# Grouped-query attention and a residual MLP on one core: where the next batch's attention is threaded into the MLP, and in what portions

## The chip, the core and the metric

The kernel runs on one core of a Trainium2 chip. Its engines run side by side, each through its own list of instructions: TensorE (PE; its weight loads are shown as PEld), VectorE (DVE), ScalarE (ACT), GpSimd (POOL) and SyncE (SP). POOL and SP issue nearly all the transfers. The metric is the device time of one launch in microseconds, as the median of several runs.

## The reference

Eight batches are independent of one another. Each is an attention with 16 query heads and 4 key/value heads (384 positions, head width 64), followed by a mixing block over positions and an MLP over 1024 channels with 4096 hidden ones.

```
attention:  scores = q @ k.T / 8 ;  attn = softmax(scores) ;  x = attn @ v      # 16 heads, 4 share one k, v
a1 = alpha1 * x + beta1
u  = x + lam * (w_tok @ a1)            # mixes the 384 positions
a2 = alpha2 * u + beta2
out = u + lam * (relu(a2 @ w_ch1) @ w_ch2)     # 1024 -> 4096 -> 1024
```

Inputs and outputs are float32; the matmul operands are bfloat16 on the chip.

## The kernel before

**The main work of a pass.** A pass b is the MLP of batch b. `main(b)` issues it as two halves. The first half is the hidden layer: 32 tiles `nt` of 128 hidden channels, each 8 matmuls of 384 columns over the input tiles `dt` (line 413), with ReLU by ACT for even tiles and by DVE for odd ones into `hT` (lines 421 and 423). Its weights come in 16 chunks of two tiles through a ring of five buffers; the load of chunk c+5 is issued by POOL when chunk c is done (line 128). The second half is the output layer: six tiles (`dw`, `ms`), each 32 matmuls of 512 columns (line 448), then two DVE operations `o` (lines 453 and 454) and a store issued by SP (line 455). Both halves use two PSUM banks with the tag "mm" in turn.

**The side work.** The attention and the mixing of batch b+1, `side(b+1)`, are cut into pieces and issued between the main matmuls of pass b. `main` is a generator: it yields after every four matmuls, and at a yield the caller may issue one piece. The pieces are, for a pair p of heads (8 pairs):

- `scores(i)`: one group of four 128x128 score tiles for both heads of a pair (line 202). 18 groups hold the batch's 72 tile pairs. The contraction is 64 wide, so the two heads use the upper and the lower 64 rows of the array. ACT takes the exponential of a whole group, 128x1024 (line 211), into one of four buffers `es`. `scores2(j)` issues two groups in one piece; the exponential of the second is put on the list `late`, which is emptied a little later.
- `av_piece(p, hh)`: the product with v for one head, nine matmuls of 65 columns (line 237). After the second head DVE takes the reciprocal of the sums and scales (lines 242 and 243), then computes a1 (lines 250 and 252).
- `tok(p)`: the mixing over positions, nine matmuls of 128 columns (line 259), and on DVE the sum u and a2 (lines 266 and 270).
- `a2_transpose(p)`: a transposing transfer, issued by SP, writes a2 into `a2T` for the next pass (line 282). For batch 1 the last two pairs go over TensorE. `tok_flip` is `tok` and this.

In the passes from the second on the pieces are spread over the whole pass: nine slots of `scores2`, 16 of `av_piece`, 8 of `tok_flip`. The rule is one line, with `span` 0.95 and `lead` 0 there: a piece is issued when its share of the list is due by the time worked off.

```
if done < len(us) and done * t_all * span < len(us) * (t - t_all * lead):
```

The PSUM for scores is a tag "sc" with two buffers of two banks each; "av" and "tp" have one bank each.

**Inputs of batch b+2.** During pass b, SP loads k at the start (`load_k`). At 55% of the pass POOL copies k into its place (line 101) and issues the loads of q and v (`load_next`, lines 110 and 105). At 85% SP issues two transposing transfers, `flip_k` into `kT` (line 113) and `flip_q` into `qT` (line 117). In the first pass the order is different: the loads for batch 2 are issued at the end of the first half, and the flips at 75%. `kT`, `qT`, the staged q and the placed k have one buffer each.

The order on every engine is the order in which the program issues; no scheduler moves anything (`manual_schedule`).

Of the kernel before, what the change touches and what calls it, by code (L numbers as in the profile page):

```python
# [12 lines left out]
def kernel(  # L13
# [21 lines left out]
    nc = tc.nc  # L35
# [12 lines left out]
    P = 128  # L48
# [14 lines left out]
    sb = ST(tc.tile_pool(name="sb", bufs=2))  # L63
    psum = ST(tc.psum_pool(name="psum", bufs=2))

# [49 lines left out]

    def flip_q(b):
        nc.sync.dma_start_transpose(out=qT.rearrange("p a j s -> p (a j) s"),
                                    in_=qrs[b].rearrange("p h st d -> p (h st d)"))

# [11 lines left out]
    def load_w2(dw, i, n):  # L131
        r, cs = slice(i * NNT // n, (i + 1) * NNT // n), slice(dw * 512, (dw + 1) * 512)
        nc.gpsimd.dma_start(out=w2[:, r, cs], in_=w2src[:, r, cs])  # L133

    def tp_ps(shape, tag="tp"):
        return psum.tile(shape, bf, tag=tag, name="tp", bufs=2 if tag == "mm" else 1)

# [8 lines left out]
    def h_part(nts, dts):  # L146
        for nt in nts:
            if nt % 2 == 0 and nt not in early:
                t = psum.tile([P, 2, 512], f32, tag="sc", name="h", bufs=2)
                early[nt], early[nt + 1] = t[:, 0], t[:, 1]  # L150
            for dt in dts:
                nc.tensor.matmul(out=early[nt][:, :S + 1], lhsT=w1_tiles[nt // CW][:, dt, nt % CW * P:(nt % CW + 1) * P],  # L152
                                 rhs=a2Ts[0][:, dt, :S + 1], start=(dt == 0), stop=(dt == NDT - 1))
# [4 lines left out]
    def side(b):  # L158
# [6 lines left out]
        first = b == 0  # L165
        pe_flip = b < 2

# [14 lines left out]
        def q_transpose(p, n=2, tag="tp", eng="DVE"):  # L182
            src = qrs[1][:, 2 * p:2 * (p + n)] if b else qgs[2 * p // G][:, 2 * p % G:2 * p % G + 2 * n]
            src = src.rearrange("p h st d -> p (h st d)")
            f = src.dtype == f32
            ps = psum.tile([P, n * NST, P], src.dtype, tag=tag, name="tp", bufs=2 if tag == "mm" else 1)
            for i in range(n * NST):
                nc.tensor.matmul(out=ps[:, i, :], lhsT=src[:, i * P:(i + 1) * P], rhs=ident_f if f else ident,
                                 is_transpose=True, start=(i == 0), stop=(i == n * NST - 1), skip_group_check=True)
            evac(eng)(out=qT[:, p:p + n].rearrange("p a j s -> p (a j) s"), in_=ps)  # L190
# [3 lines left out]
        def scores(i, later=False):  # L194
            sc = psum.tile([P, 2, 4, P], f32, tag="sc", name="sc", bufs=2)
            k = 4 * i
            while k < 4 * i + 4:
                n = min(4 * i + 4, k - k % NST + NST) - k
                p, sk, st = k // (NST * NST), k // NST % NST, k % NST
                for hh in range(2):  # L200
                    r = slice(hh * D, (hh + 1) * D)
                    nc.tensor.matmul(out=sc[:, hh, k % 4:k % 4 + n], lhsT=kT[r, sk, 2 * p // G, :],  # L202
                                     rhs=qT[r, p, st:st + n, :], start=True, stop=True)
                k += n

            def exp():
                if first:
                    e = hTf[:, i % 6 * 1024:(i % 6 + 1) * 1024].rearrange("p (h k s) -> p h k s", h=2, k=4)
                else:
                    e = sb.tile([P, 2, 4, P], bf, tag="es", name="es", bufs=EB)  # L210
                nc.scalar.activation(out=e, in_=sc, func=EXP, scale=scale_qk)  # L211
                ess[i] = e

            if later:
                late.append(exp)
            else:
                exp()

        def scores2(j):
# [3 lines left out]
            scores(2 * j + 1, True)  # L223

        def av_piece(p, hh):
            while late:
                late.pop(0)()
            if hh == 0:
                avs[p] = psum.tile([P, 2, NST, D1], f32, tag="mm" if first else "av", name="av",
                                   bufs=2 if first else 1)  # L230
            av = avs[p]
# [22 lines left out]
        def tok(p):  # L254
            tag, n = ("mm", 2) if first else ("av", 1) if pe_flip else ("tp", 1)
            ps = psum.tile([P, NST, P], f32, tag=tag, name="tok", bufs=n)
            for tt in range(NST):
# [14 lines left out]
        def a2_transpose(p):  # L272
            if first:
                ps = psum.tile([P, NST, P], f32, tag="tp" if p % 2 else "av", name="ut", bufs=1)
                for tt in range(NST):
                    nc.tensor.matmul(out=ps[:, tt, :], lhsT=x[:, tt, cols(p)], rhs=ident_f, is_transpose=True,
                                     start=(tt == 0), stop=(tt == NST - 1), skip_group_check=True)
                nc.scalar.activation(out=a2T[:, p, :S], in_=ps.rearrange("p a b -> p (a b)"),
                                     func=mybir.ActivationFunctionType.Copy, scale=al2T[:, p:p + 1])
                return  # L280
            if not pe_flip or p < 6:
                nc.sync.dma_start_transpose(
# [21 lines left out]
        def rows_r(tag):  # L304
            ps = psum.tile([P, 512], f32, tag=tag, name="r", bufs=1)
            for st in range(NST):
# [13 lines left out]
        def spread(ps_, vs, tag, eng="DVE"):  # L320
            n = len(ps_)
            ps = psum.tile([P, 4, P], f32, tag=tag, name="vec", bufs=1)
            w = vs[1] - vs[0]
# [8 lines left out]
        def add(f, *a):  # L332
            us.append(lambda: f(*a))

        def tok_flip(p):
            tok(p)
            a2_transpose(p)

        if not first:
            if pe_flip:  # L340
                add(split, 2, 4)
                add(k_transpose, 0)
                add(q_transpose, 0, 2, "av")
                add(k_transpose, 2)
                add(q_transpose, 2, 2, "av")
            for j in range(NP + 4):
# [3 lines left out]
                if j <= NP:  # L350
                    add(scores2, j)
                    if pe_flip and j in (1, 3):
                        add(q_transpose, 4 + 2 * (j // 2))
                if 2 < j < NP + 3:
                    add(tok if pe_flip else tok_flip, j - 3)
                if pe_flip and j > 3:
                    add(a2_transpose, j - 4)
                if pe_flip and j < 2:
# [3 lines left out]
                elif j < 2:  # L362
                    us.extend([lambda: None] * 2)
            return us
# [4 lines left out]
        lower, upper = range(NP // 2), range(NP // 2, NP)  # L369
        def av(p):  # L370
            av_piece(p, 0)
            av_piece(p, 1)

        ut = a2_transpose
# [27 lines left out]
    def main(b):  # L402
# [3 lines left out]
        for c in range(NCH):  # L406
            w1 = w1_tiles.pop(b * NCH + c)
            for j in range(CW):
                nt = c * CW + j
                begun = b == 0 and nt in early  # L410
                ps = early[nt] if begun else psum.tile([P, 512], f32, tag="mm", name="h", bufs=2)
                for dt in range(0 if begun else NDT):
# [27 lines left out]
        for dw in range(NDW):  # L440
            cs = slice(dw * 512, (dw + 1) * 512)
            for ms in range(NST):
                ps = psum.tile([P, 512], f32, tag="mm", name="ch", bufs=2)
                o = sb.tile([P, 512], f32, tag="tmp", name="o", bufs=4)
# [16 lines left out]
    with tc.manual_schedule(engines=order):  # L461

        def warmup(n):
            warm = psum.tile([P, 512], f32, tag="mm", name="warm", bufs=2)
            for _ in range(n):
# [97 lines left out]
        for b in range(B):  # L563
            us = side(b + 1) if b + 1 < B else []
            half = False
            done, t, loaded, flipped = 0, 0, b == 0 or b + 2 >= B, b + 2 >= B
            lead, span = (0.04, 0.82) if b == 0 else (0, 0.95)
            if b + 2 < B:
                load_k(b + 2)
            for dt in main(b):  # L570
                t += dt
                half = not half
                if late and half:
                    late.pop(0)()
                if done < len(us) and done * t_all * span < len(us) * (t - t_all * lead):
                    us[done]()
                    done += 1
                if not loaded and t > t_all * 0.55:
                    loaded = True
                    load_next(b + 2)  # L580
                if not flipped and t > t_all * (0.85 if b else 0.75):
                    flipped = True
                    flip_k(b + 2)
                    flip_q(b + 2)
            while done < len(us):
                us[done]()
                done += 1


# [28 lines left out]
```

The softmax here doesn't subtract the row's maximum and nothing guards it: scores larger than these inputs give would overflow.

## Time and profile before

| | us |
|---|---|
| median of 7 runs | 811.53 (810.67 to 813.43) |
| the profiled execution: device time | 814.55 |
| its span, first to last instruction | 812.4 |
| PE busy | 797.9 (98% of the span) |
| DVE, ACT, POOL busy | 343.6, 226.1, 178.0 |
| DMA engines, mean busy share by 40ths of the span | mostly 90% or more, less in the second half of each pass |

The profiled execution took 2.15 us more than its span, and 3.02 us more than the median of the runs. A pass from the third to the sixth takes 97.4 us in the trace; the last one, which has no side work, 84.5 us from its first matmul to the end of the table's window. The granted TensorE clock has a mean of 0.998.

### The profile page before, as it was taken

Reading aid. Unit: us, or ns where it says so; the run is one execution under the profiler, and the core shown is the slowest. Engines: PE = TensorE matmul, PEld = TensorE weight load, DVE = VectorE, ACT = ScalarE, POOL = GpSimd, SP = SyncE. Lnnn points to the kernel's source line nnn. Section 1 sums busy time; section 2 is a strip of 40 time slices with the busy share of each in tenths; the row PEclk is TensorE's granted clock in tenths of the full one; section 3 lists DMA queues with packets and bytes.
Section 4 is the critical chain, followed back from the end, with each engine's and each line's share of the span. In section 5 each row is a group of like instructions: output and inputs, shape, how many; then the busy total and the mean of one; then the engine's idle time right before and its main releaser. Section 6 shows DMA issues by size and latency. Waiting matters only on the chain.

```text
span 812.4 us, 14107 instructions
## 1 busy us (share of the span) xinstructions
PE 797.9 (98%) x6076; PEld 450.6 (55%) x6129; DVE 343.6 (42%) x669; ACT 226.1 (28%) x311; POOL 178.0 (22%) x232
## 2 busy tenths in 40 slices
PE   8999999999999999999999999999999999999997
PEld 4766554565456654566455655556545565456545
DVE  7645552344433444344452444424444244432122
ACT  6654211332113321233103331034211432102100
POOL 6234320324002330123201340022500321003000
PEclk9999999999999999999999999999999999999999
DMA  9999999999169992799947997499935999129611
GB/s 186 197 207 200 205 200 185 155 170 167 36 137 182 178 134 69 137 171 170 127 96 129 173 180 87 113 141 163 188 69 103 154 173 127 37 66 184 88 40 40
DMA packets 233550, 112.96 MB, mean 139 GB/s; under 512 B 82952, under 2 KB 227344, under 8 KB 233488
## 3 DMA queue, kind: packets, MB, share of 16 engines
q0 software_dynamic: 170736, 83.47, 82.8%
q1 hardware_dynamic: 62208, 28.20, 15.4%
q8 instruction: 48, 0.79, 0.4%
q10 hardware_dynamic: 544, 0.39, 0.1%
q14 instruction: 14, 0.11, 0.1%
HBM read 170.53 MB, written 12.58 MB: 225 GB/s over the span
## 4 chain that ended last, share of the span: by engine, by line
PE 85%; DMA 9%; DVE 4%; issue 1%; POOL 1%; ACT 0%; SPq 0%; POOLq 0%; DVEq 0%
PE h L413 36%; PE ch L448 36%; DMA w<-in_moe_w_ch_dram 6%; PE av L237 4%; PE sc L202 4%; PE tok L259 4%; DMA q_raw<-in_q_dram 2%; DVE x L243 1%; DVE hT L423 1%; PE h L152 1%; DMA a2T<-a 1%; DVE a1f L250 0%; DVE a L252 0%; PE warm L466 0%; POOL w L133 0%
## 5 line engine op out<-in xcount | busy, mean ns | idle before, releaser
L413 PE MATMUL h<-a2T,w 128*128 128x384 bf16 (+1 forms) x2016 | 351.4, 327 | 1.0 <-DVE hT L423 0.3
L448 PE MATMUL ch<-w,hT 128*128 128x512 bf16 (+2 forms) x1547 | 345.3, 370 | 4.3 <-issue 1.0
L413 PEld LDWEIGHTS <-w 128*128 128x128 bf16 x2016 | 190.0, 98 | 126.9 <-issue 10.7
L448 PEld LDWEIGHTS <-hT 128*128 128x128 bf16 x1600 | 146.3, 98 | 154.1 <-issue 5.8
L128 POOL DMA_DIRECT2D w<-in_moe_w_ch_dram x128 | 112.3, 879 | 542.2 <-PE h L413 504.7
L211 ACT ACTIVATE es<-sc 128x1024 bf16<-128x1024 f32 x126 | 123.4, 1021 | 290.9 <-PE sc L202 290.9
L423 DVE TENSOR_SCALAR hT<-h,bias 128x384 bf16<-128x384 f32 x128 | 79.0, 617 | 190.7 <-PE h L413 190.1
L421 ACT ACTIVATE hT<-h,bias 128x384 bf16<-128x384 f32 x128 | 74.3, 581 | 204.8 <-PE h L413 204.3
L453 DVE TENSOR_TENSOR o<-ch,vecs 128x512 f32<-128x512 f32 (+2 forms) x50 | 33.3, 666 | 91.1 <-PE ch L448 91.1
L266 DVE TENSOR_TENSOR x<-tok,x 128x384 f32<-128x384 f32 x64 | 35.5, 555 | 80.2 <-PE tok L259 77.9
L237 PEld LDWEIGHTS <-es 128*128 128x128 bf16 x1008 | 45.8, 97 | 20.5
L237 PE MATMUL av<-v,es 128*128 128x65 bf16 x1008 | 49.0, 193 | 0.0
L202 PE MATMUL sc<-qT,kT 64*128 64x384 bf16 (+2 forms) x576 | 45.7, 273 | 1.7 <-DMA qT<-q_raw 1.6
L259 PEld LDWEIGHTS <-wtokT 128*128 128x128 bf16 x576 | 37.8, 98 | 13.8 <-DVE x L243 1.6
L242 DVE RECIPROCAL rinv<-av 128x6 f32<-128x6 f32 x64 | 12.3, 192 | 71.1 <-PE av L237 70.9
L259 PE MATMUL tok<-a,wtokT 128*128 128x128 bf16 x504 | 37.3, 219 | 0.0
L243 DVE TENSOR_TENSOR x<-av,rinv 128x384 f32<-128x384 f32 x64 | 35.7, 557 | 2.2
L202 PEld LDWEIGHTS <-kT 64*128 64x128 bf16 x576 | 19.9, 94 | 29.6 <-issue 25.1
L454 DVE TENSOR_TENSOR o<-o,x 128x512 f32<-128x512 f32 (+2 forms) x50 | 33.5, 670 | 1.7
L270 DVE TENSOR_TENSOR a<-x,vecs 128x384 bf16<-128x384 f32 x56 | 31.6, 565 | 1.9
L252 DVE TENSOR_TENSOR a<-a1f,vecs 128x384 bf16<-128x384 f32 x56 | 31.4, 561 | 2.2
L250 DVE TENSOR_TENSOR a1f<-x,vecs 128x384 f32<-128x384 f32 x56 | 31.4, 561 | 1.9
(75 smaller groups left out, 195.6 us busy)
## 6 DMA issues: line engine op xcount, KB each, us to landing
w<-in_moe_w_ch_dram POOLq DMA_DIRECT2D x138, 512.0 KB, 8.0
out_dram<-o SPq DMA_DIRECT2D x47, 256.0 KB, 2.4
q_raw<-in_q_dram POOLq DMA_DIRECT2D x28, 192.0 KB, 7.1
kst<-in_k_dram SPq DMA_DIRECT2D x16, 192.0 KB, 3.4
w<-in_moe_w_ch_dram POOLq DMA_DIRECT2D x1, 2048.0 KB, 16.8
v<-in_v_dram POOLq DMA_DIRECT2D x24, 64.0 KB, 6.8
w<-in_moe_w_ch_dram POOLq DMA_DIRECT2D x4, 256.0 KB, 10.4
a2T<-a SPq DMA_TRANSPOSE x54, 2.3
```

The source lines that it names most:

```text
L128: nc.gpsimd.dma_start(out=t, in_=w1src[:, :, c * CW * P:(c + 1) * CW * P])
L202: nc.tensor.matmul(out=sc[:, hh, k % 4:k % 4 + n], lhsT=kT[r, sk, 2 * p // G, :], rhs=qT[r, p, st:st + n, :], start=True, stop=True)
L211: nc.scalar.activation(out=e, in_=sc, func=EXP, scale=scale_qk)
L237: nc.tensor.matmul(out=av[:, hh, sq, :], lhsT=ess[k // 4][:, m % 2, k % 4, :], rhs=vb[:, sk, hk, :], start=(sk == 0), stop=(sk == NST - 1))
L243: nc.vector.tensor_tensor(out=x[:, :, cols(p)].rearrange("p st (h d) -> p h st d", h=2), in0=av[:, :, :, :D], in1=rinv.to_broadcast([P, 2, ...
L259: nc.tensor.matmul(out=ps[:, tt, :], lhsT=wtokT[:, st, tt * P:(tt + 1) * P], rhs=a1s[p][:, st, :], start=(st == 0), stop=(st == NST - 1 an ...
L266: nc.vector.tensor_tensor(out=u, in0=ps, in1=u, op=ADD)
L413: nc.tensor.matmul(out=ps[:, :n], lhsT=w1[:, dt, j * P:(j + 1) * P], rhs=a2T[:, dt, :n], start=(dt == 0), stop=(dt == NDT - 1))
L421: nc.scalar.activation(out=hT[:, nt, :], in_=ps[:, :S], func=RELU, bias=c1)
L423: nc.vector.tensor_scalar(out=hT[:, nt, :], in0=ps[:, :S], scalar1=c1, scalar2=0.0, op0=ADD, op1=mybir.AluOpType.max)
L448: nc.tensor.matmul(out=ps[:, lo:hi], lhsT=hT[:, nt, ms * P:(ms + 1) * P], rhs=w2[:, nt, dw * 512 + lo:dw * 512 + hi], start=(nt == 0), sto ...
L454: nc.vector.tensor_tensor(out=o[:, lo:hi], in0=o[:, lo:hi], in1=x[:, ms, c], op=ADD)
```

## The change

For the side work issued in the second and the later passes (the batches from 2 on):

- Nothing is issued in the first half of the pass. From the end of the first half on, the yields are numbered by u (48 more in the six output tiles), and a table tells which pieces stand at which u.
- `scores3` issues three groups in one piece, so there are six slots of scores. In two of the six, the third group's exponential is held back until after the following `av`.
- `av` issues both heads of a pair in one piece, so there are eight slots. `tok_flip` keeps its eight; one of them stands directly behind an `av`.
- The PSUM banks "sc", "av" and "tp" are given back after the first pass and become one ring "threes" of three buffers of two banks. Scores, `av` and `tok` take its buffers in turn.
- `load_k` stands at u=1, `load_next` at u=2, `flip_k` at u=34, and `flip_q` is four transfers of two pairs each at u=36, 37, 42 and 43.

The first pass is as before. The core of the diff:

```diff
-    psum = ST(tc.psum_pool(name="psum", bufs=2))
+    mms = ST(tc.psum_pool(name="mms", bufs=2))
+    lead_banks = ExitStack()
+    psum = lead_banks.enter_context(tc.psum_pool(name="psum", bufs=2))
+    threes = []
...
-    def flip_q(b):
-        nc.sync.dma_start_transpose(out=qT.rearrange("p a j s -> p (a j) s"),
-                                    in_=qrs[b].rearrange("p h st d -> p (h st d)"))
+    def flip_q(b, i=0, n=NP):
+        nc.sync.dma_start_transpose(out=qT[:, i:i + n].rearrange("p a j s -> p (a j) s"),
+                                    in_=qrs[b][:, 2 * i:2 * (i + n)].rearrange("p h st d -> p (h st d)"))
...
+    def three():
+        return threes[0].tile([P, 2, 4, P], f32, tag="sc", name="sc", bufs=3)
...
-            sc = psum.tile([P, 2, 4, P], f32, tag="sc", name="sc", bufs=2)
+            sc = bank([P, 2, 4, P], "sc", "sc") if b < 2 else three()
...
+        def scores3(i, later=False):
+            for k in range(3):
+                scores(3 * i + k, later and k == 2)
+
         def av_piece(p, hh):
-            while late:
+            while late and b < 2:
                 late.pop(0)()
             if hh == 0:
-                avs[p] = psum.tile([P, 2, NST, D1], f32, tag="mm" if first else "av", name="av",
-                                   bufs=2 if first else 1)
+                if b < 2:
+                    avs[p] = bank([P, 2, NST, D1], "mm" if first else "av", "av")
+                else:
+                    avs[p] = three()[:, 0].rearrange("p k s -> p (k s)")[:, :2 * NST * D1].rearrange(
+                        "p (h st d) -> p h st d", h=2, st=NST)
...
-            tag, n = ("mm", 2) if first else ("av", 1) if pe_flip else ("tp", 1)
-            ps = psum.tile([P, NST, P], f32, tag=tag, name="tok", bufs=n)
+            ps = bank([P, NST, P], "mm" if first else "av", "tok") if b < 2 else three()[:, 0, :NST]
...
+        def av(p):
+            av_piece(p, 0)
+            av_piece(p, 1)
+            if b > 1:
+                while late:
+                    late.pop(0)()
...
+        if b > 1:
+            return {0: [(scores3, 0)], 4: [(av, 0)], 6: [(scores3, 1)], 8: [(tok_flip, 0)], 11: [(av, 1)],
+                    13: [(scores3, 2, True)], 15: [(av, 2)], 16: [(tok_flip, 1)], 18: [(tok_flip, 2)], 19: [(av, 3)],
+                    21: [(scores3, 3)], 23: [(tok_flip, 3)], 25: [(av, 4)], 27: [(scores3, 4)], 29: [(tok_flip, 4)],
+                    31: [(av, 5)], 33: [(scores3, 5, True)], 35: [(av, 6), (tok_flip, 5)], 37: [(av, 7)],
+                    39: [(tok_flip, 6)], 41: [(tok_flip, 7)]}
...
+            if b == 0:
+                load_k(2)
+            elif b + 2 < B:
+                for u, f, *a in ((1, load_k), (2, load_next), (34, flip_k), (36, flip_q, 0, 2), (37, flip_q, 2, 2),
+                                 (42, flip_q, 4, 2), (43, flip_q, 6, 2)):
+                    us.setdefault(u, []).append((f, b + 2, *a))
...
+                elif t >= 2 * NNT * T_H:
+                    for f, *a in us.get(u, []):
+                        f(*a)
+                    u += 1
+            if b == 0:
+                assert done == len(us)
+                lead_banks.close()
+                threes.append(ST(tc.psum_pool(name="threes", bufs=3)))
```

`bank(...)` takes the tag "mm" from the pool `mms` and the other tags from `psum`, with the sizes that the calls had before.

More of the change, by code (lines that the diff above doesn't have):

```diff
@@ L133, in load_w2, with bank @@
         nc.gpsimd.dma_start(out=w2[:, r, cs], in_=w2src[:, r, cs])
+    def bank(shape, tag, name, dtype=f32):
+        if tag == "mm":
+            return mms.tile(shape, dtype, tag="mm", name=name, bufs=2)
+        return psum.tile(shape, dtype, tag=tag, name=name, bufs=2 if tag == "sc" else 1)
+    def three():
+        return threes[0].tile([P, 2, 4, P], f32, tag="sc", name="sc", bufs=3)
     def tp_ps(shape, tag="tp"):
-        return psum.tile(shape, bf, tag=tag, name="tp", bufs=2 if tag == "mm" else 1)
+        return bank(shape, tag, "tp", bf)
     late = []
@@ L148, in h_part @@
             if nt % 2 == 0 and nt not in early:
-                t = psum.tile([P, 2, 512], f32, tag="sc", name="h", bufs=2)
+                t = bank([P, 2, 512], "sc", "h")
                 early[nt], early[nt + 1] = t[:, 0], t[:, 1]
@@ L165, in side @@
         first = b == 0
-        pe_flip = b < 2
         def cols(p):
@@ L185, in q_transpose @@
             f = src.dtype == f32
-            ps = psum.tile([P, n * NST, P], src.dtype, tag=tag, name="tp", bufs=2 if tag == "mm" else 1)
+            ps = bank([P, n * NST, P], tag, "tp", src.dtype)
             for i in range(n * NST):
@@ L273, in a2_transpose @@
             if first:
-                ps = psum.tile([P, NST, P], f32, tag="tp" if p % 2 else "av", name="ut", bufs=1)
+                ps = bank([P, NST, P], "tp" if p % 2 else "av", "ut")
                 for tt in range(NST):
@@ L280, in a2_transpose @@
                 return
-            if not pe_flip or p < 6:
+            if b > 1 or p < 6:
                 nc.sync.dma_start_transpose(
@@ L304, in rows_r @@
         def rows_r(tag):
-            ps = psum.tile([P, 512], f32, tag=tag, name="r", bufs=1)
+            ps = bank([P, 512], tag, "r")
             for st in range(NST):
@@ L321, in spread @@
             n = len(ps_)
-            ps = psum.tile([P, 4, P], f32, tag=tag, name="vec", bufs=1)
+            ps = bank([P, 4, P], tag, "vec")
             w = vs[1] - vs[0]
@@ L337, in tok_flip @@
             a2_transpose(p)
-        if not first:
[L340 to L345, printed above, removed]
+        if b > 1:
[4 more added lines that the diff above has]
+                    39: [(tok_flip, 6)], 41: [(tok_flip, 7)]}
+        if not first:
+            add(split, 2, 4)
+            add(k_transpose, 0)
+            add(q_transpose, 0, 2, "av")
+            add(k_transpose, 2)
+            add(q_transpose, 2, 2, "av")
             for j in range(NP + 4):
@@ L351, in side @@
                     add(scores2, j)
-                    if pe_flip and j in (1, 3):
+                    if j in (1, 3):
                         add(q_transpose, 4 + 2 * (j // 2))
                 if 2 < j < NP + 3:
-                    add(tok if pe_flip else tok_flip, j - 3)
-                if pe_flip and j > 3:
+                    add(tok, j - 3)
+                if j > 3:
                     add(a2_transpose, j - 4)
-                if pe_flip and j < 2:
+                if j < 2:
                     for p in (4 * j, 4 * j + 2):
@@ L361, in side @@
                     add(spread, range(4 * j, 4 * j + 4), (3, 4), "tp", "ACT")
-                elif j < 2:
-                    us.extend([lambda: None] * 2)
             return us
@@ L369, in side @@
         lower, upper = range(NP // 2), range(NP // 2, NP)
-        def av(p):
-            av_piece(p, 0)
-            av_piece(p, 1)
         ut = a2_transpose
@@ L410, in main @@
                 begun = b == 0 and nt in early
-                ps = early[nt] if begun else psum.tile([P, 512], f32, tag="mm", name="h", bufs=2)
+                ps = early[nt] if begun else bank([P, 512], "mm", "h")
                 for dt in range(0 if begun else NDT):
@@ L442, in main @@
             for ms in range(NST):
-                ps = psum.tile([P, 512], f32, tag="mm", name="ch", bufs=2)
+                ps = bank([P, 512], "mm", "ch")
                 o = sb.tile([P, 512], f32, tag="tmp", name="o", bufs=4)
@@ L463, in warmup @@
         def warmup(n):
-            warm = psum.tile([P, 512], f32, tag="mm", name="warm", bufs=2)
+            warm = bank([P, 512], "mm", "warm")
             for _ in range(n):
@@ L563 @@
         for b in range(B):
-            us = side(b + 1) if b + 1 < B else []
+            us = side(b + 1) if b + 1 < B else {}
             half = False
[L566 to L569, printed above, removed]
+            done, t = 0, 0
+            if b == 0:
[4 more added lines that the diff above has]
+                    us.setdefault(u, []).append((f, b + 2, *a))
@@ L570 @@
+            flipped = False
+            u = 0
             for dt in main(b):
                 t += dt
[L572 to L584, printed above, removed]
@@ L585 @@
-            while done < len(us):
-                us[done]()
-                done += 1
+                if b == 0:
+                    half = not half
+                    if late and half:
+                        late.pop(0)()
+                    if done < len(us) and done * t_all * 0.82 < len(us) * (t - t_all * 0.04):
+                        us[done]()
+                        done += 1
+                    if not flipped and t > t_all * 0.75:
+                        flipped = True
+                        flip_k(2)
+                        flip_q(2)
+                elif t >= 2 * NNT * T_H:
+                    for f, *a in us.get(u, []):
+                        f(*a)
+                    u += 1
@@ L591 @@
+            if b == 0:
+                assert done == len(us)
+                lead_banks.close()
+                threes.append(ST(tc.psum_pool(name="threes", bufs=3)))
 _INS = ['q', 'k', 'v', 'moe_alpha1', 'moe_beta1', 'moe_w_tok', 'moe_alpha2', 'moe_beta2', 'moe_w_ch1', 'moe_w_ch2', 'moe_lam']
```

## The prediction

> **What bounds the kernel now.** The page comes first, for the engine that is never free; then the chain of waits by engine.
>
> ```profile
> PE 797.9 (98%) x6076; PEld 450.6 (55%) x6129; DVE 343.6 (42%) x669; ACT 226.1 (28%) x311; POOL 178.0 (22%) x232
> PE 85%; DMA 9%; DVE 4%; issue 1%; POOL 1%; ACT 0%; SPq 0%; POOLq 0%; DVEq 0%
> ```
>
> TensorE is busy for 98% and carries 85% of the chain, so an edit counts by the TensorE time it removes or the stall it makes. Next, busy time by stretch: a middle pass, then the last pass up to its final tiles.
>
> ```profile
> 335.95:433.39 97.44, 96.87 (x731) 54.08 (x738) 41.21 (x77) 26.31 (x35) 21.01 (x27) 1.00 1.00 138
> 724.50:809.00 84.50, 83.35 (x509) 47.32 (x510) 19.63 (x33) 9.30 (x16) 9.62 (x11) 1.00 0.58 90
> ```
>
> The columns are length, busy PE, PEld, DVE, ACT, POOL, clock, DMA share, GB/s. In a middle pass PE idles 0.57 us in 97.44: there is no stall to win back, only the cost of issuing the side work. That is read from TensorE's timeline (start, duration), since a duration holds pipeline latency, but the next group's start does not:
>
> ```profile
> 335.34 0.61 PE L202 MATMUL sc<-qT,kT 64*128 64x384 bf16 x8
> 335.88 6.02 PE L413 MATMUL h<-a2T,w 128*128 128x384 bf16 x36
> 341.84 0.61 PE L202 MATMUL sc<-qT,kT 64*128 64x128 bf16 x8
> 342.38 6.67 PE L413 MATMUL h<-a2T,w 128*128 128x384 bf16 x40
> 348.89 0.43 PE L237 MATMUL av<-v,es 128*128 128x65 bf16 x9
> 349.17 2.76 PE L413 MATMUL h<-a2T,w 128*128 128x384 bf16 x16
> ```
>
> From 342.38 to 348.89 are 40 hidden matmuls, 0.1625 us each. The 36 from 335.88 should end at 341.73, but the scores start at 341.84 and the next hidden matmul at 342.38: a slot of two score groups costs 342.38 - 341.73 = 0.65, 0.64 in most slots. An av slot costs 349.17 - 348.88 = 0.28, and a tok slot, read the same way, 0.50. So 32 x 8 x 0.1625 + 192 x 0.2158 (the same reading of the output half) + 9 x 0.64 + 16 x 0.28 + 8 x 0.50 = 97.3, against 97.44.
>
> In the first pass, single groups of scores and whole pairs of av stand beside other work:
>
> ```profile
> 15.46 0.39 PE L202 MATMUL sc<-qT,kT 64*128 64x128 bf16 x4
> 15.78 0.66 PE L307 MATMUL r<-wtokT,stage 128*32 128x384 bf16 x3
> ...
> 32.23 0.71 PE L237 MATMUL av<-v,hT 128*128 128x65 bf16 x18
> 32.78 0.52 PE L276 MATMUL ut<-hT,x 128*128 128x128 f32 x3
> ```
>
> One group takes 0.32 from its start to the next start, two take 0.54: a further group costs 0.22, and of 0.64 about 0.64 - 2 x 0.215 = 0.21 belongs to the slot, not to its groups. A whole pair of av takes 0.55, as much as two halves.
>
> **What the skill says.** The Trainium skill, "TensorEngine Tiling (Array Packing)", Key Properties: changing the tiling mode drains TensorE. The trace agrees. Only scores use the 64-row mode, and the waits show their weight loads held back once per slot (waited in all, times, longest), 0.36 us each:
>
> ```profile
> PEld L202 <- issue: 25.1, 69, 1.6
> ```
>
> "TensorE: Matmul & The Clock Gate", Part 1: the clock is halved after a free-running window of about 3.4 us with too little work. The trace has this once, at the start of the second pass:
>
> ```profile
> 136.05 0.81 PE L413 MATMUL h<-a2T,w 128*128 128x384 bf16 x4
> 138.49 0.61 PE L202 MATMUL sc<-qT,kT 64*128 64x384 bf16 x8 [1.62 <-DMA qT<-q_raw]
> 139.03 7.99 PE L413 MATMUL h<-a2T,w 128*128 128x384 bf16 x36
> 146.95 0.61 PE L202 MATMUL sc<-qT,kT 64*128 64x128 bf16 x8
> ```
>
> The 36 matmuls from 139.03 took 7.92 instead of 5.85 us, 2.07 more.
>
> **The change, part by part.**
>
> *Scores in threes.* Six slots of 0.21 + 3 x 0.215 = 0.855 make 5.13 us; nine of 0.64 made 5.76. Saved: **0.63 us a pass**. Ends for the unknown slot of three: 0.75 if most of the switch hides, and 0.96 if the cost goes by groups; that is 1.26 to 0 us a pass. I take 0.63, the increment between one group and two.
>
> *Whole pairs of av, tok behind av.* 0.55 against 2 x 0.28: nothing, at most 0.15 us a pass either way.
>
> *From the first half to the second.* Score slots between output matmuls also cost 0.64 (392.26 to 392.90), av 0.28, tok 0.50: nothing. The instructions are the same in number, with the flip of q excepted.
>
> *Cover in the second half.* A u is four output matmuls, 0.863 us. Exponentials start 0.49 after a score slot and follow each other every 0.92, so the third ends at 0.49 + 1.84 + 1.02 = 3.35. The av after four u starts at 0.76 + 3.45 = 4.21: 0.86 to spare. The tightest places are tok 5, straight behind av 6 at u=35: its buffer's exponential ends 2.43 after the slot at u=33 starts, it starts at 0.76 + 1.73 + 0.55 = 3.04, 0.6 to spare; and av 7, whose held-back exponential ends about 1.3 us after av 6, 0.9 to spare. The third group of a slot needs the buffer of the av before it, which DVE has scaled about 1 us after that av ended; the group comes 2.2 us after. DVE does about 8 x 2.99 (lines 242 to 252, 266, 270) + 6 x 1.38 (lines 453, 454) = 32 us in 54, so it keeps up.
>
> *Inputs.* POOL waits for k at u=2 with only the loads of q and v behind it; the next weight load on its queue comes in the next pass. SP issues four flips of q for one. A flip of three blocks takes SP 1.18 us and the whole q about 3.8, so four pieces cost perhaps 5 instead of 3.8, on a queue with gaps. The last a2T flip (u=41) stands ahead of the last two pieces. It waits for DVE: 1.4 for the output tile in front, 1.1 of its own, 2.3 to land, 5.3 us with latencies. Seven u (6.0) and seven hidden matmuls (1.1) pass before it is read.
>
> *The first half alone.* It now looks like the last pass, which ran 256 hidden matmuls without a wait. Its weight chunks landed in:
>
> ```profile
> DMA to landing us min/median/max: 5.6/6.6/8.2
> ```
>
> A chunk may take 4 x 2.6 = 10.4 us.
>
> *The start of the second pass.* SP's order up to there is unchanged: the flip of q, then the fifth a2T flip. The scores that waited until 138.49 leave this place, but the chain shows the a2T flip ending at 139.45, and the sixth hidden matmul (dt=5) needs it. So this stall stays, and the slow clock with it. The first score slot lay in its shadow and now costs: 8 x 0.64 against 6 x 0.855 is nothing in this pass.
>
> *Sum.* Five passes (third to seventh) x 0.63 = 3.15 us, and the second 0 in the profiled execution: 814.55 - 3.15 = 811.4. That execution stands 3.02 above the median of the runs, about the size of the stall, so the stall may be smaller in other runs; then the second pass also saves, 3.8 in all. I take 3.4: 811.53 - 3.4 = **808.1**.
>
> **Rivals.** 0.2% (1.6 us) is about what a measurement of this kernel can tell from no change.
>
> *No change* (811.0): threes cost 0.96, or stalls of some 0.5 us a pass eat the gain: the spare 0.6 us behind ACT is thin, as buffers of scores, av and tok now wait for each other. Against: 0.32 and 0.54 for one and two groups.
>
> *Slower*: the weight ring in the bare first half. A chunk is used every 2.6 us instead of about 3.0, and a middle pass showed
>
> ```profile
> DMA to landing us min/median/max: 5.9/8.7/9.8
> ```
>
> If chunks land later than 10.4 us, TensorE waits. A wait of 1.0, which with a slow window costs 2.07 more, in five passes gives 811.5 - 3.15 + 15.4 = 823.8; it decides from about 0.6 us of wait a pass. For it: the DMA share, taken over 5 us at a time, is above 1.3 through most of the last pass's first half. Against: the last pass at the same pace, and k, q, v and the a2T flips leave this half.
>
> *The change only moves things* (810.9): half of the switch hides already, 0.1 us a pass. That lies in the no-change case.
>
> *Larger gain* (805.5): the switch is mostly hidden in threes, 1.0 us saved in each of six passes, or the stall of the second pass shrinks.
>
> **How the numbers follow.** Forecast 0.70, no change 0.14, weights late or another stall over 0.8 us a pass 0.10, larger gain 0.06. The range from 805.5 to 811.5 takes in the larger gain and the no-change case and leaves out the slow one. Faster by over 0.2%: 0.70 + 0.06 = 0.76; within 0.2%: 0.14; slower: 0.10.
>
> **What would show it.** Right: middle passes of 96.8 us, score slots of 12 matmuls that cost 0.85, 51 weight-load waits at line 202 instead of 69 (69 - 6 x 9 + 6 x 6), a first half of 41.6 us, the stall near 137 still there. Wrong: PE idle before av or tok for ACT, idle at hidden matmuls for w, or a slot of 0.96.

## The result, and the profile after

The changed kernel takes **807.22 us** (median of 13 runs, 805.41 to 810.80) against 811.38 us for the kernel before (32 runs): a ratio of 0.9953, 95% interval 0.9942 to 0.9963, so 3.0 to 4.7 us less. Forecast were 808.1 us and a gain of 3.4. The profiled execution took 806.72 us with a span of 804.9.

The page of the changed kernel, engines first and then the chain of waits by engine:

```profile
PE 789.7 (98%) x6064; PEld 452.0 (56%) x6129; DVE 341.9 (42%) x669; ACT 227.9 (28%) x311; POOL 177.6 (22%) x232
PE 88%; DMA 9%; DVE 2%; issue 1%; ACT 0%; SPq 0%; POOLq 0%
```

TensorE still sets the time. It is busy for 8.2 us less, with the same instructions (the counts differ by records that the traces lack). Busy time by stretch, for a middle pass and the last one up to its final tiles (length, PE, PEld, DVE, ACT, POOL, clock, DMA share, GB/s):

```profile
330.29:426.94 96.65, 95.87 (x728) 54.47 (x736) 40.95 (x76) 26.63 (x34) 21.01 (x27) 1.00 0.93 139
716.88:801.40 84.52, 83.41 (x509) 47.35 (x511) 19.62 (x32) 9.28 (x16) 9.62 (x11) 1.00 0.58 90
```

A middle pass is 0.80 us shorter than the 97.44 of before; 96.8 was forecast. Its idle time on PE is not shorter (96.65 - 95.87 = 0.78 us against 0.57): since the ends of matmuls are modelled, the gain has to be read from their starts. The last pass has not changed. TensorE's timeline of that pass shows the slots:

```profile
330.29 41.76 PE L439 MATMUL h<-a2T,w 128*128 128x384 bf16 x256
371.99 0.83 PE L214 MATMUL sc<-qT,kT 64*128 64x384 bf16 x12
372.75 3.63 PE L474 MATMUL ch<-w,hT 128*128 128x512 bf16 x15
...
384.17 0.70 PE L257 MATMUL sc<-v,es 128*128 128x65 bf16 x18
384.71 1.89 PE L474 MATMUL ch<-w,hT 128*128 128x512 bf16 x7
```

The 256 hidden matmuls run in one piece. They should end at 330.29 + 256 x 0.1625 = 371.89; the next main matmul starts at 372.75, so twelve score matmuls, three groups, cost 0.86 us. A pair of av costs 0.54 to 0.55. (av and tok now stand in the score ring, so the trace names their output `sc`; the line tells them apart.) The weight loads of the scores are held back less often, 48 times instead of 69 (51 was forecast):

```profile
PEld L214 <- issue: 17.8, 48, 0.4
```

The start of the second pass, on TensorE:

```profile
136.11 0.98 PE L439 MATMUL h<-a2T,w 128*128 128x384 bf16 x5
137.81 12.51 PE L439 MATMUL h<-a2T,w 128*128 128x384 bf16 x76 [0.73 <-DMA a2T<-a]
```

The sixth hidden matmul waits for the fifth a2T flip, as forecast, but for 0.73 us, and the clock stays at full speed. Between the two profiled executions this pass went from 101.1 to 97.5 us; 2.0 of these 3.6 us are not the change, as the second trace of the kernel before shows below, and how much of the rest is the change is not known. The chunks of w in the bare first half of a middle pass landed in:

```profile
DMA to landing us min/median/max: 6.0/8.0/8.8
```

### The profile page after: what moved, and what is told of

Same layout as the page of the kernel before. It is cut to its first block, busy times and chain, and to the rows that moved or that the text cites. A ratio compares the mean times of both kernels' runs of the same rounds, so it can differ in the third digit from the quotient of the medians.

```text
span 804.9 us, 14140 instructions
## 1 busy us (share of the span) xinstructions
PE 789.7 (98%) x6064; PEld 452.0 (56%) x6129; DVE 341.9 (42%) x669; ACT 227.9 (28%) x311; POOL 177.6 (22%) x232
## 4 chain that ended last, share of the span: by engine, by line
PE 88%; DMA 9%; DVE 2%; issue 1%; ACT 0%; SPq 0%; POOLq 0%
PE h L439 38%; PE ch L474 36%; DMA w<-in_moe_w_ch_dram 6%; PE sc L214 4%; PE sc L257 3%; PE sc L278 3%; DMA q_raw<-in_q_dram 2%; PE h L165 1%; PE tok L278 1%; PE av L257 1%; PE warm L492 0%; DMA a2T<-a 0%; PE ut L295 0%; DVE hT L561 0%; PE tp L200 0%
## 5 line engine op out<-in xcount | busy, mean ns | idle before, releaser
L439 PE MATMUL h<-a2T,w 128*128 128x384 bf16 (+1 forms) x2016 | 333.7, 327 | 1.0 <-DMA a2T<-a 0.7
L439 PEld LDWEIGHTS <-w 128*128 128x128 bf16 x2016 | 195.5, 98 | 131.0 <-issue 2.0
L474 PEld LDWEIGHTS <-hT 128*128 128x128 bf16 x1600 | 144.5, 98 | 153.1 <-issue 9.6
L257 PEld LDWEIGHTS <-es 128*128 128x128 bf16 x1008 | 39.3, 97 | 14.3
L278 PEld LDWEIGHTS <-wtokT 128*128 128x128 bf16 x576 | 37.4, 98 | 13.7 <-DVE x L263 1.7
L214 PE MATMUL sc<-qT,kT 64*128 64x384 bf16 (+2 forms) x576 | 42.4, 272 | 1.1 <-ACT qT L202 0.2
L285 DVE TENSOR_TENSOR x<-sc,x 128x384 f32<-128x384 f32 x48 | 26.5, 552 | 32.2 <-PE sc L278 31.6
L262 DVE RECIPROCAL rinv<-sc 128x6 f32<-128x6 f32 x48 | 9.3, 193 | 66.1 <-PE sc L257 66.1
L257 PE MATMUL sc<-v,es 128*128 128x65 bf16 x864 | 34.2, 193 | 0.0
L278 PE MATMUL sc<-a,wtokT 128*128 128x128 bf16 x432 | 32.0, 219 | 0.3
L263 DVE TENSOR_TENSOR x<-sc,rinv 128x384 f32<-128x384 f32 x48 | 26.7, 557 | 1.6
```

Source lines behind the costliest of these rows:

```text
L257: nc.tensor.matmul(out=av[:, hh, sq, :], lhsT=ess[k // 4][:, m % 2, k % 4, :], rhs=vb[:, sk, hk, :], start=(sk == 0), stop=(sk == NST - 1))
L278: nc.tensor.matmul(out=ps[:, tt, :], lhsT=wtokT[:, st, tt * P:(tt + 1) * P], rhs=a1s[p][:, st, :], start=(st == 0), stop=(st == NST - 1 an ...
L439: nc.tensor.matmul(out=ps[:, :n], lhsT=w1[:, dt, j * P:(j + 1) * P], rhs=a2T[:, dt, :n], start=(dt == 0), stop=(dt == NDT - 1))
L474: nc.tensor.matmul(out=ps[:, lo:hi], lhsT=hT[:, nt, ms * P:(ms + 1) * P], rhs=w2[:, nt, dw * 512 + lo:dw * 512 + hi], start=(nt == 0), sto ...
```

## Experiments

Passes are measured in the traces from the first hidden matmul of one to that of the next. Ratios are to the kernel before, run on the same chip; on the chip of the last three rows it took 811.9 us, with single runs up to 816.3.

| kernel | median, us | ratio (95% interval) | middle pass, us | second pass, us |
|---|---|---|---|---|
| before (first trace) | 811.38 | | 97.44 | 101.1 |
| before (second trace) | 812.5, one run | | 97.45 | 99.1 |
| changed | 807.22 | 0.9953 (0.9942 to 0.9963) | 96.65 | 97.5 |
| score groups two and one | 814.41 | 1.0037 (1.0022 to 1.0052) | 97.92 | 104.3 |
| twos, all in the second half | 812.02 | 1.0005 (0.9986 to 1.0023) | 97.45 | 98.0 |
| the same, one tok later | 810.71 | 0.9991 (0.9980 to 1.0002) | 97.29 | 98.6 |
| threes over the whole pass | 826.54 | 1.0179 (1.0143 to 1.0215) | 99.97 | 103.7 |
| before, ReLU of tile 23 on ACT | 810.19 | 0.9981 (0.9970 to 0.9992) | 97.29 | 101.5 |
| inputs where they were | 807.72 | 0.9956 (0.9941 to 0.9972) | 96.65 | 96.6 |
| flips of batch 2 in the second pass | 814.34 | 1.0036 (1.0023 to 1.0049) | 96.65 | 104.1 |
| changed, again | 806.82 | 0.9930 (0.9907 to 0.9953) | 96.65 | 97.7 |
| flips of batch 2 at 88% | 805.79 | 0.9910 (0.9887 to 0.9934) | 96.65 | 97.0 |
| the same, q in four pieces | 805.80 | 0.9913 (0.9892 to 0.9934) | 96.65 | 96.65 |

**Does a slot of scores have a fixed cost?** The third group goes to the next u.

```diff
-            for k in range(3):
-                scores(3 * i + k, later and k == 2)
+            for k in range(2):
+                scores(3 * i + k)
+        def third(i, later=False):
+            scores(3 * i + 2, later)
-            return {0: [(scores3, 0)], 4: [(av, 0)], 6: [(scores3, 1)], ...
+            return {0: [(scores3, 0)], 1: [(third, 0)], 4: [(av, 0)], 6: [(scores3, 1)], 7: [(third, 1)], ...
```

> The changed kernel with the third group of each score slot issued one u later, so that the same 18 groups stand in 12 slots (six of two, six of one). Theory S (a slot of scores has a fixed cost, whatever it holds): six slots of 0.639 and six of about 0.425 instead of six of 0.857 us, 1.24 us more a pass, 7.5 us in six passes: 814.7 us, slower than the kernel before by 3.3. Rival G (the cost goes by groups, the gain comes from where the side work stands): no change, 807.2 us.

Measured: 814.41 us, a middle pass 1.27 longer than the changed kernel's, as theory S had it (1.24). Its timeline:

```profile
378.94 0.61 PE L214 MATMUL sc<-qT,kT 64*128 64x384 bf16 x8
379.48 1.04 PE L478 MATMUL ch<-w,hT 128*128 128x512 bf16 x3
380.45 0.39 PE L214 MATMUL sc<-qT,kT 64*128 64x128 bf16 x4
380.78 2.76 PE L478 MATMUL ch<-w,hT 128*128 128x512 bf16 x12
```

Four output matmuls were issued from 379.48 on (one record is missing), which end at 380.34; the next one starts at 380.78. So the slot of one group costs 0.44 by these rounded starts, and 0.42 in each of the six slots, taken from the last main matmul before to the first one after. One, two and three groups cost 0.42, 0.64 and 0.857: about 0.20 for the slot and 0.218 for each group. Rival G falls. The slots of `av` have no such fixed cost (0.276 for one head, 0.55 for two), so it belongs to the scores; that it is the change of the row mode fits this, but no run here issued scores in another mode.

**The move alone.** The changed kernel with nine slots of two, all in the second half. (Besides the table, the exponential of a slot's second group is no longer held back, but for the last slot.)

```diff
-            return {0: [(scores3, 0)], 4: [(av, 0)], 6: [(scores3, 1)], ...
+            return {0: [(scores2, 0)], 2: [(scores2, 1)], 5: [(av, 0)], 6: [(scores2, 2)], 8: [(tok_flip, 0)], 11: [(av, 1)],
+                    13: [(scores2, 3)], 15: [(av, 2)], 16: [(tok_flip, 1)], 17: [(scores2, 4)], 18: [(tok_flip, 2)],
+                    20: [(av, 3)], 22: [(scores2, 5)], 23: [(tok_flip, 3)], 25: [(av, 4)], 27: [(scores2, 6)],
+                    29: [(tok_flip, 4)], 31: [(av, 5)], 33: [(scores2, 7)], 34: [(scores2, 8, True)],
+                    36: [(av, 6), (tok_flip, 5)], 38: [(av, 7)], 39: [(tok_flip, 6)], 41: [(tok_flip, 7)]}
```

> The changed kernel with nine slots of two score groups, as many as before, but all of them in the second half like the rest of the side work. Theory S: the move alone keeps only the 0.165 us wait of one hidden matmul for a ReLU on DVE and 0.03 of the av pairs, about 0.2 us a pass; so 6 x 0.61 = 3.7 us are lost against the changed kernel: about 810.9 us, 0.5 to 1.2 below the kernel before. Rival P (the place makes the gain): within 1 us of the changed kernel, 807.2 to 808.2.

Measured: 812.02 us and passes of 97.45, as long as before. Nothing of the gain is left, so rival P falls. But theory S had 0.2 us a pass too little, and 0.15 of it is one of the eight tok slots, which costs 0.65 instead of 0.50. In this kernel's timelines of TensorE, ACT and DVE (of ACT the first exponential of the slot at u=17 alone):

```profile
393.71 1.04 PE L474 MATMUL ch<-w,hT 128*128 128x512 bf16 x4
394.73 0.66 PE L278 MATMUL sc<-a,wtokT 128*128 128x128 bf16 x9
```

```profile
393.66 1.02 ACT L223 ACTIVATE es<-sc 128x1024 bf16<-128x1024 f32 x1 [3.22 <-PE sc L214]
```

```profile
394.26 0.55 DVE L285 TENSOR_TENSOR x<-sc,x 128x384 f32<-128x384 f32 x1
```

The four output matmuls from 393.71 end at 394.57; the tok starts at 394.73. The expectation below takes this for a wait for the buffer of the tok before it, whose sum is line 285. That does not fit: the sum ends at 394.81, after the tok has started. What ends just before it, at 394.68, is the exponential of the first score group of u=17, and the program as built gives this tok the PSUM buffer of that group (in the changed kernel the three buffers do come strictly in turn). One u later should end this wait too:

```diff
-                    ... 17: [(scores2, 4)], 18: [(tok_flip, 2)],
+                    ... 17: [(scores2, 4)], 19: [(tok_flip, 2)],
```

> The kernel with nine slots of two score groups in the second half, with the third tok (u=18) one u later. In its trace a middle pass took 97.45 us, because that tok waited 0.15 us for the PSUM buffer of the tok before it, whose DVE sum stands behind an output tile's two operations. If so: that slot falls from 0.65 to 0.50 us, a pass takes 97.30, 0.9 us less than with u=18. If the move as such brings nothing: 97.45 again.

Measured: passes of 97.29 us, 0.16 less, as expected, though the expectation named the wrong engine: the tok now starts 0.76 us after that exponential has ended, and waits for nothing. The ratio went from 1.0005 to 0.9991, with intervals that overlap. So the move alone is worth about 0.15 us a pass, if its own table adds no wait.

**What the move removes.** In the trace of before one of nine score slots costs 0.804 us instead of 0.639, at the same place in each pass. Two views of that place, DVE and TensorE:

```profile
371.50 0.56 DVE L252 TENSOR_TENSOR a<-a1f,vecs 128x384 bf16<-128x384 f32 x1
371.98 0.61 DVE L423 TENSOR_SCALAR hT<-h,bias 128x384 bf16<-128x384 f32 x1
```

```profile
371.93 0.61 PE L202 MATMUL sc<-qT,kT 64*128 64x128 bf16 x8
372.64 2.11 PE L413 MATMUL h<-a2T,w 128*128 128x384 bf16 x12
```

The ReLU of tile 23 (line 423) stands on DVE behind the a1 operations of an av and ends at 372.59; tile 25 uses the same PSUM bank and starts at 372.64. (The scores seem to end at 372.54, so only 0.10 of this wait of 0.165 shows as idle time.) The edit to the kernel before:

```diff
-                if nt % 2 == 0:
+                if nt % 2 == 0 or nt == 23 and 0 < b < B - 1:
                     nc.scalar.activation(out=hT[:, nt, :], in_=ps[:, :S], func=RELU, bias=c1)
```

> The kernel before with the ReLU of hidden tile 23 on ACT instead of DVE in the passes that have spread side work after the first one. In the trace of before one score slot a pass costs 0.804 instead of 0.639 us, and the matmul after it waits for DVE. If that is a wait for tile 23's ReLU behind the a1 operations of an av: the slot falls to 0.64, 0.165 x 6 = 1.0 us less, 810.4. If it is only a gap in the records: no change, 811.4.

```profile
371.06 0.61 PE L202 MATMUL sc<-qT,kT 64*128 64x128 bf16 x8
371.60 2.13 PE L413 MATMUL h<-a2T,w 128*128 128x384 bf16 x12
```

The next hidden matmul now starts 0.54 after the scores, not 0.71. Passes fell to 97.29, the time by 0.1 to 0.3%: the wait was real.

**Threes without the move.** The changed slots over the whole pass, inputs as before.

```diff
-                elif t >= 2 * NNT * T_H:
-                    for f, *a in us.get(u, []):
-                        f(*a)
-                    u += 1
+                while keys and t >= t_all * keys[0] / 46:
+                    for f, *a in us[keys.pop(0)]:
+                        f(*a)
```

> The changed kernel's slots (six of three score groups, pairs of av, the ring of three PSUM buffers) spread over the whole pass instead of its second half; k, q and v are loaded and flipped where the kernel before does it. Theory S alone: slots of 0.857 also between hidden matmuls, 6 x 0.61 = 3.7 below the kernel before: 807.7. Theory S with a second term that the second half hides: three exponentials (2.85 us) stand in front of the ReLU of the next even tile on ACT, and a PSUM bank of the hidden layer is wanted again after 1.3 us; with waits of 0 to 1.9 us, say 1, at three slots a pass: 18 us more, some 826. The rival that the place is neutral expects 807.7.

Measured: 826.54 us, as the theory with waits behind ACT had it. The slots cost 0.855 to 0.859 here too, but hidden matmuls wait 3.3 us a pass in four places: three for a ReLU on ACT behind exponentials (2.5 us together), one for a ReLU on DVE behind the a1 operations of an av pair (0.8). One of the three, in the timeline of TensorE and ACT:

```profile
353.04 0.83 PE L214 MATMUL sc<-qT,kT 64*128 64x384 bf16 x12
...
353.53 2.85 ACT L223 ACTIVATE es<-sc 128x1024 bf16<-128x1024 f32 x3 [1.76 <-PE sc L214]
...
353.80 2.12 PE L439 MATMUL h<-a2T,w 128*128 128x384 bf16 x12
...
356.26 0.59 ACT L447 ACTIVATE hT<-h,bias 128x384 bf16<-128x384 f32 x1
...
356.91 2.11 PE L439 MATMUL h<-a2T,w 128*128 128x384 bf16 x12 [0.98 <-ACT hT L447]
```

Three exponentials hold ACT to 356.38, the ReLU behind them ends at 356.85, and the tile that wants its bank starts at 356.91. So with this division of the ReLUs between ACT and DVE, threes pay only in the second half, where there are none. Whether another division would let them pay in the first half was not tried.

**The inputs.** Everything for batch b+2 back to about where it was, q in one piece.

```diff
-                for u, f, *a in ((1, load_k), (2, load_next), (34, flip_k), (36, flip_q, 0, 2), (37, flip_q, 2, 2),
-                                 (42, flip_q, 4, 2), (43, flip_q, 6, 2)):
+                load_k(b + 2)
+                for u, f, *a in ((5, load_next), (34, flip_k), (34, flip_q)):
```

> The changed kernel with k loaded at the start of the pass, q and v at u=5, and k and q flipped at u=34, q in one transfer. The theory that the inputs are not on the path: middle passes of 96.65 us as in the changed kernel, 807.2 us. The rival that their place or the four pieces give part of the gain: 0.1 us a pass or more, over 807.8.

Measured: 807.72 us, ratio 0.9956 against 0.9953, and middle passes of 96.65, but for one of 96.86. Inputs and pieces bring nothing that can be measured.

**The start of the second pass.** The kernel before, once more:

> The kernel before once more, for a second trace of the start of its second pass. Theory W: the middle passes take 97.44 us again; the second pass takes 101.1 us where the clock falls to a half after the wait for the flips, and about 99 or less where it does not, and the time follows it: 814.5 or some 811 us.

Its second trace, on TensorE:

```profile
136.09 0.81 PE L413 MATMUL h<-a2T,w 128*128 128x384 bf16 x4
138.21 0.61 PE L202 MATMUL sc<-qT,kT 64*128 64x384 bf16 x8 [1.30 <-DMA qT<-q_raw]
138.75 6.30 PE L413 MATMUL h<-a2T,w 128*128 128x384 bf16 x36
```

The wait is there, the slow clock is not (6.24 us to the next slot, not 7.92), and the pass takes 99.1 us. In the first trace the clock is at half (0.50, third column from the end) for 3.4 us:

```profile
139.90:143.30 3.40, 3.40 (x13) 1.58 (x12) 0.46 (x1) 1.60 (x3) 0.20 (x1) 0.50 0.41 134
```

So the slow clock alone cost 7.92 - 6.24 = 1.68 us; the prediction's 2.07 also held 0.39 us in which the clock had no part, most of it the wait for the a2T flip. The run took 812.5 us, 0.8 above the median of the kernel before on this chip, so the median run may wait less; no trace of such a run exists. But the mean clock is on record for every run. Of the 13 runs of the changed kernel, the three with a mean clock below 0.999 took 809.85 to 810.80 us and the ten others 805.41 to 807.93. Of the 51 runs of the kernel before on the chip of the first experiment, the nine below 0.999 took 813.44 to 818.33 and the others 809.84 to 813.01. Not every run fits (the kernel before once took 811.01 us at 0.997), but a fall of the clock goes with most of the long times of both kernels. Where it fell is known only for the traces, and there it is always in the second pass. The forecast had the pass neutral because the a2T flip landed at 139.45 in the first trace of before; its landing swings with the run (TensorE waited for it until 137.81 in the changed kernel, until 139.61 in the kernel with groups two and one).

The wait comes from SP, where the flip of q for batch 2 stands for 13 us ahead of that a2T flip, in the changed kernel too:

```profile
120.53 12.98 SPq L122 DMA_TRANSPOSE qT<-q_raw  x1
133.60 0.53 SPq L481 DMA_DIRECT2D out_dram<-o  x1
134.19 1.20 SPq L301 DMA_TRANSPOSE a2T<-a  x1
```

First attempt to take it away:

```diff
-                    if not flipped and t > t_all * 0.75:
-                        flipped = True
-                        flip_k(2)
-                        flip_q(2)
...
+            if b == 1:
+                flip_k(2)
+                flip_q(2)
```

> The changed kernel with the flips of k and q for batch 2 issued at the start of the second pass instead of at 75% of the first; their scores come only in the second half of the second pass. In the trace of the changed kernel the flip of q holds SP for 12.98 us in front of the fifth a2T flip, and the sixth hidden matmul of the second pass waits 0.73 us for that flip. Theory W (this wait, and in some runs the slow clock after it, is what spreads the changed kernel's times from 805.4 to 810.8 us): no wait, a second pass of 96.65 instead of 97.54 us, 805.8 us median, and no runs near 810. Rival: the flips land among the weight chunks of the bare first half, and TensorE waits for w there: 807 us or more.

Measured: 814.34 us, 0.36% slower than before. The first wait is gone, but the second pass takes 104.1. SP's timeline, the landing of that half's chunks, and the waits of the pass (in all, times, longest):

```profile
138.63 10.49 SPq L122 DMA_TRANSPOSE qT<-q_raw  x1
```

```profile
DMA to landing us min/median/max: 9.7/11.2/15.8
```

```profile
PEld L439 <- DMA w<-in_moe_w_ch_dram: 7.5, 7, 2.8
PE h L439 <- DMA w<-in_moe_w_ch_dram: 4.9, 4, 2.5
```

Theory W was wrong in this form and its rival right: this is the prediction's slower case, made to happen. A chunk may take 10.4 us, these took up to 15.8, and the clock halved once as well. The flips belong between: behind the fifth a2T flip and ahead of the next chunks.

```diff
-                    if not flipped and t > t_all * 0.75:
+                    if not flipped and t > t_all * 0.88:
```

> The changed kernel with the flips of k and q for batch 2 at 88% of the first pass instead of 75%: behind the fifth a2T flip on SP, and ahead of the second pass's weight chunks. Theory W in its corrected form (the fifth a2T flip must not stand behind the flip of q, and the flip of q must not run beside the chunks of a bare first half): a second pass of 96.65 us, 805.8 us median, few runs above 808. The rival: the flip of q still runs at 138 us, beside the first chunks, which then land after more than 10.4 us: the second pass takes over 98 us.

```diff
+                    if not flipped and t > t_all * 0.88:
                         flipped = True
                         flip_k(2)
-                        flip_q(2)
+                        todo = [0, 2, 4, 6]
+                    elif flipped and todo and t > t_all * (0.97 - 0.02 * len(todo)):
+                        flip_q(2, todo.pop(0), 2)
```

> As the kernel with the flips for batch 2 at 88%, but q in four pieces at 89, 91, 93 and 95% of the first pass. If the flip of q is bound by the transfers in flight and not by its length, the second pass and the time are those of the one-piece version, 96.65 and 805.8 us; if the gaps keep the a2T tiles and chunks flowing, it is the one version without a long wait when the other has one.

> The changed kernel once more, on the same chip as the two versions with later flips for batch 2. All theories: middle passes of 96.65 us and 807.2 us, with a second pass between 96.6 and 100 us by the length of the wait for the fifth a2T flip.

Measured on one chip: 805.79 (804.81 to 806.20), 805.80 (805.61 to 806.03) and, for the changed kernel, 806.82 us (806.45 to 809.39), six runs each. The twelve runs with later flips all have a mean clock of 0.999 or more, so theory W in its corrected form holds, and these two are the fastest versions. SP's timeline and the landings, first with q in one piece, then in four:

```profile
132.92 4.00 SPq L122 DMA_TRANSPOSE qT<-q_raw  x1
```

```profile
DMA to landing us min/median/max: 6.7/9.8/10.3
```

```profile
133.07 5.44 SPq L122 DMA_TRANSPOSE qT<-q_raw  x4
```

```profile
DMA to landing us min/median/max: 7.1/7.6/8.1
```

At 10.3 us the chunks are at the limit: there the second pass is 0.4 us longer, as weight loads wait for w four times; with four pieces it is not. The medians of the two are the same.

## Why the prediction was right

- **What bounds the kernel**: right but for one statement. "There is no stall to win back" in a middle pass was wrong: one hidden matmul waited 0.165 us for DVE, and the modelled ends of matmuls hid part of it. The list of slots came to 97.3 against 97.44, and the missing 0.14 was, within its rounding, the trace of it; only the most common cost of a score slot had been read, not all nine.
- **Scores in threes**: right, 0.857 against 0.855, extrapolated from one group and two. 9 x 0.639 - 6 x 0.857 = 0.61 us a pass, against 0.63.
- **Pairs of av**: 0.55 against 2 x 0.276, as said.
- **From the first half to the second**: costed at nothing; it is worth 0.15 to 0.165 a pass, the wait for DVE that it removes. This is the mis-sized term: 0.80 a pass instead of 0.63, five times 0.17, so 0.85 us more than the 3.15 forecast for these passes. (0.61 and 0.165 leave 0.025 of the 0.80 unexplained.)
- **Cover in the second half**: no wait in the middle passes, so the 0.6 us of room behind ACT was enough. The kernel with twos shows how near the ring of three buffers is to a wait for ACT: a tok moved by 0.86 us decides over 0.15.
- **The first half alone**: right, with chunks landing within 8.8 us. The slower rival was a true danger at the point given for it, as the flips among the chunks showed; the slow clock in its sum was priced at 2.07 us and cost 1.68.
- **The second pass**: the mechanism was right (the a2T flip behind the flip of q, still waited for), the size was not: 0.73 us, no slow clock. The gain of the median, 4.2 us, is 5 x 0.80 from the other passes and about 0.2 left for this one. That this lies next to the 0.25 that the forecast had allowed (3.4 - 3.15) is luck: in the traces the pass is 1.6 or 3.6 us shorter, by which trace of before one takes, as the "larger gain" rival had it, and the landing of that flip swings from run to run. What the change does to this pass in the median run stays open.

## What to carry to other kernels

A visit to the 64-row scores costs about 0.20 us here, whatever it holds, so such small matmuls belong together in as large portions as PSUM takes. How large they can be is set by the engine that empties them: three exponentials in a row cost nothing where ACT is free, and made TensorE wait 2.5 us a pass where ACT also has ReLUs to do, so the place and the portion must be chosen together. When a sum of slot costs falls short of the measured pass, read every slot, not the usual one: a few tenths are a wait on some queue. And before naming the queue, check that the work blamed had ended when the wait did.

## What was not expected of the hardware

A transposing transfer of q (24 blocks) holds SP for 3.6 to 4.7 us where it is issued in one piece in the second or a later pass. At 75% of the first pass it took 12.4 to 13.7 us in ten traces, at 88% of it 4.0, and beside the weight chunks at the start of the second pass 10.5, while their landing went from 8.5 to 11.2 us in the median. The DMA engines' share was 1.39 during the one of 12.98 us and 1.14 during the one of 4.0; that the traffic beside it makes the difference fits this and was not tested by itself. In four pieces at the end of the first pass it took 5.4 us of SP and left the landings of the following chunks at most 8.1, against 10.3 with one piece; each comes from one trace.

The prediction speaks of a window of about 3.4 us with too little work; here waits well short of 3.4 us were enough to halve the clock. Between the first 8 us and the last matmul, five of the thirteen traces have a wait of TensorE longer than 1.5 us (1.62, 2.45, 2.73, 3.23 and 3.64). In each of them the clock goes to half, during the wait or up to 1.4 us after its end, for 3.41 us, in the last for twice that. The waits from 0.7 to 1.43 us in the thirteen traces, some forty, were not followed by it.
